# A Fourier filter and an expert layer on one core: three of eight sequences take their first-stage sums through DRAM

## The chip, the core and the metric

The kernel runs on one NeuronCore of a Trainium2 chip. The metric is the device time of one execution in microseconds. The kernel before took 454.48 us (the median of three runs, 452.73 to 454.86).

## The reference

The first half is a filter along the sequence, by Fourier transform; the second is a layer of experts that each keep at most 80 tokens.

```python
# x: 8 sequences x 2496 positions x 256 channels, f32; filt: 1249 x 256, complex
X = np.fft.rfft(x, axis=1)
y = np.fft.irfft(X * (filt_r + 1j * filt_i)[None], n=2496, axis=1)

x = y.reshape(19968, 256)
logits = x @ w_gate                          # 8 experts
expert_idx = argmax(logits); gate_w = its softmax probability
out = zeros((19968, 256))
for e in range(8):
    tok = the (at most 80) tokens of expert e with the largest gate_w
    out[tok] = gate_w[tok] * (relu(x[tok] @ w1[e]) @ w2[e])     # 256 -> 1024 -> 256
```

At most 640 of the 19968 rows of the output are not zero.

## The kernel before

Everything is float32 and runs on one core: TensorE for products and transposes, ScalarE and VectorE to take results out of the accumulators (PSUM), VectorE and GpSimd for the product with the filter. SyncE issues most DMAs, ScalarE's queue some, GpSimd's the gathers. The order of work is written out by hand in one loop (`tc.manual_schedule()`, from L824); each engine then works through its own instructions in order, and starts each as soon as what it waits for is there. SyncE computes nothing and runs ahead until a wait holds it.

The transform of length 2496 = 39 x 64 is done in two stages, and the kernel goes back only as far as it must: the gate's logits are worked out from the spectrum, and only the rows that are picked are turned back into tokens.

- **Stage 1** (`stage1`, L317) works on sequence `b` in 11 groups `k`. Line `j*21+g` of the 64 (j of 0 to 2, g of 0 to 20) is transformed over its 39 positions; three lines (the three values of j) go into one product by a block table `wf_t` of 117 x 120. A group has two such g, so four products: x is the stationary side (117 x 128 channels, twice), `wf_t` the moving one (120 columns). Group 10 has one g. Line 63 does not fit this order; for three sequences at once it is worked out with group 10 of sequences 0, 3 and 6, and kept in `left`. The results lie with channels on partitions and are copied into `t1` (L332), 80 x 64 to a channel, written with 64 floats between neighbours.
- **Transposes** (`transpose1`, L341): for each of 10 parts `u` of a sequence, four transposes turn `t1` so that lines and (real, imaginary) lie on partitions; ScalarE copies the result (`t2`, L349). They are issued `LEAD` = 2 steps ahead.
- **Stage 2** (`stage2`, L353): four products with the table `d_t` (L358), then two VectorE products with the filter `ft` (L366) and two GpSimd additions (L373).
- **Turn** (`turn`, L381): `LATE` = 2 steps later, four products with `gi` (identity and gate weights side by side, 136 columns, L386) turn the spectrum and give its gate sums; ScalarE copies it (L402).
- **Spectra kept** (`keep_spectrum`, L377): two parts at a time are stored to the DRAM tensor `yf` from ScalarE's queue, 512 KB each, five stores a sequence and 40 in all; those of sequence 0 go out one during each of sequences 1 to 5. The spectra of sequences 0 and 1 also stay in SBUF (`ysb`).
- **Zeros** (`put_zeros`, L194): 64 stores of 312 KB from SyncE fill the whole output with zeros. Only the scatter of the experts at the end depends on them.

One step `v` of the loop (L908) is part `u` of sequence `b`, with v = 10 b + u. It issues stage 2 of v, loads of x whose buffers are free (`put_x`, 7 buffers), the transposes of v + 2, one or two groups of stage 1 of a later part (`put_s1`), for the first sequence a transpose of the filter (`turn_filter`), a store of zeros, and the turn of v - 2. `fps` is a rotation of three PSUM buffers shared by stage 1, transposes and stage 2; `t1pool` holds two `t1`; `t2pool` has four buffers.

After the 80 steps come the choice of tokens, the turning back of the chosen rows (`turn_rows`, `add_rows`, which reload spectra from `yf`) and the experts (`Experts`), none of which the change edits. Two passes on TensorE make one f32 product, so counts in the profile are twice the products; a transpose is one pass.

Of the kernel before, what the change touches and what calls it, by code (L numbers as in the profile page):

```python
# [13 lines left out]
F32 = mybir.dt.float32  # L14
BF16 = mybir.dt.bfloat16
# [8 lines left out]
B, S, C = 8, 2496, 256  # L24
N = B * S
N1, N2 = 39, 64
NS, NQ = 20, 64
NU = NS // 2

NJ, NG = 3, 21  # L30
NB = NG // 2 + 1
JC = 4
# [9 lines left out]
def dft_tables():  # L42
    n1, n2 = np.arange(N1), np.arange(N2)
    s, q = np.arange(NS), np.arange(NQ)
    ph = 2 * np.pi * (np.outer(n1, s) % N1) / N1
    w = np.stack([np.cos(ph), -np.sin(ph)], 1)
    wf = np.zeros((N1, NJ, NJ, NS, 2))
    for j in range(NJ):
        wf[:, j, j] = w.transpose(0, 2, 1)

    k = np.array([[next(m for m in range(i, S, N1) if m % NQ == j) for j in q] for i in s])
    th = 2 * np.pi * (n2[:, None, None] * k % S) / S
    c, sn = np.cos(th), np.sin(th)
    d = np.zeros((2, N2, NS, 2, NQ))
    d[0, :, :, 0], d[1, :, :, 0] = c, sn
    d[0, :, :, 1], d[1, :, :, 1] = -sn, c

    two = np.where(s == 0, 1.0, 2.0) / S
    be = 2 * np.pi * (np.outer(q, n2) % NQ) / NQ
    back = np.zeros((2, NQ, 2, N2))  # L60
    back[0, :, 0], back[1, :, 0] = np.cos(be), -np.sin(be)
    back[0, :, 1], back[1, :, 1] = np.sin(be), np.cos(be)
    wi = np.zeros((4, SP, 2, N1, 4))
    for e in range(4):
        wi[e, :NS, 0, :, e] = (two * np.cos(ph)).T
        wi[e, :NS, 1, :, e] = (-two * np.sin(ph)).T

    n = (39 * n2[:, None] + 64 * n1) % S
    al = 2 * np.pi * (n.reshape(S, 1, 1) * k % S) / S
    rows = np.stack([np.cos(al), -np.sin(al)], 2) * two[:, None, None]  # L70

    frow = np.minimum(k, S - k).reshape(NU, 128).T
    fsig = np.where(k > S // 2, -1.0, 1.0).reshape(NU, 128).T
    f32 = np.float32
    return (wf.reshape(NJ * N1, -1).astype(f32), wi.reshape(4 * SP, 2, 4 * N1).astype(f32),
            d.reshape(128, NS, 128).astype(f32), back.reshape(128, 128).astype(f32),
            rows.reshape(S, NS * 128).astype(f32),
            np.ascontiguousarray(frow).astype(np.int32), np.ascontiguousarray(fsig).astype(f32))

# [2 lines left out]
def kernel(  # L82
# [11 lines left out]
    nc = tc.nc  # L94
# [10 lines left out]
    frow_dram = nc.inline_tensor(frow_host, name="frow_tbl")  # L105
    fsig_dram = nc.inline_tensor(fsig_host, name="fsig_tbl")

    NX = -(-max(E * cap - 128, 0) // 128)

    consts = ctx.enter_context(tc.tile_pool(name="consts", bufs=1))  # L110
    dpool = ctx.enter_context(tc.tile_pool(name="dram", bufs=1, space=DRAM))

    warm = consts.tile([128, 128], BF16, name="warm")
    nc.vector.memset(warm[:], 0.0)
    ident = consts.tile([128, 128], F32, name="ident")
    make_identity(nc, ident)
    ident_bf = consts.tile([128, 128], BF16, name="ident_bf")
# [16 lines left out]

    KC, KR = 8, 16
    PB, BB = 4096, 1 << 19
    K0 = K1 = 12
    cand = consts.tile([128, B, KC], F32, name="cand")  # L140
    cidx = consts.tile([128, B, KC], mybir.dt.uint32, name="cidx")
    code = consts.tile([128, B, KC], F32, name="code")
    cbase = consts.tile([128, B, KC], F32, name="cbase")
# [38 lines left out]

    NE, NY, NO = 3, 2, 3
    NWARM = 9
    yf = {b: dpool.tile([128, NS, C], F32, name=f"yf_{b}") for b in range(B)}
    ypool = ctx.enter_context(tc.tile_pool(name="spec", bufs=NY))
    ysb = {}
# [52 lines left out]
    with ExitStack() as actx:  # L240
# [17 lines left out]
        fspool = pool("fs", 3, within=bctx)  # L258
        ppool = pool("pp", 2, within=bctx)

        wf_t = tpool.tile([NJ * N1, NJ * 2 * NS], F32, name="wf_t")
        d_t = tpool.tile([128, NS, 128], F32, name="d_t")
        e_t = lpool.tile([128, 2 * N2], F32, name="e_t")
        wi_t = lpool.tile([4 * SP, 2, 4 * N1], F32, name="wi_t")
# [17 lines left out]
        def sign_filter(v):  # L282
            f = fst[:, v]
            for i in range(2):
                nc.scalar.activation(out=f[:, 2 + i, :], in_=f[:, 2 + i, :], func=AF.Copy,
                                     scale=fsig[:, 2 * v + i:2 * v + i + 1])
# [28 lines left out]
            st["x", b, ch] = xt  # L315

        def stage1(b, k):  # L317
            if k == 0:
                st["t1", b] = t1pool.tile([128, 4 * NS, N2], F32, name=f"t1_{b}", tag="t1")
            xt = st["x", b, 2 * k // JC]  # L320
            ps = fps.tile([128, 2, NJ, 4 * NS], F32, name=f"pa_{b}_{k}", tag="f")
            nk = 2 if k < NB - 1 or b % NJ == 0 else 1
            for i in range(nk):
                for cb in range(NDB):
                    nc.tensor.matmul(  # L325
                        out=ps[:, i, :, 2 * NS * cb:2 * NS * cb + 2 * NS],
                        lhsT=xt[0:NJ * N1, (2 * k + i) % JC, 128 * cb:128 * cb + 128],
                        rhs=wf_t[:], start=True, stop=True)
            full = 2 if k < NB - 1 else 1
            t1 = st["t1", b][:, :, 0:NJ * NG].rearrange("p a (j g) -> p g j a", j=NJ)  # L330
            copy = nc.vector.tensor_copy if b == 0 and k % 3 == 1 else nc.scalar.copy
            copy(out=t1[:, 2 * k:2 * k + full], in_=ps[:, 0:full])  # L332
            if k == 0 and b % NJ:
                nc.gpsimd.tensor_copy(out=st["t1", b][:, :, N2 - 1],
                                      in_=st["left"][:, b - min(b - b % NJ, B - NJ)])
            elif k == NB - 1 and b % NJ == 0:
                nc.scalar.copy(out=st["t1", b][:, :, N2 - 1], in_=ps[:, 1, b - min(b, B - NJ)])
                st["left"] = tpool.tile([128, NJ, 4 * NS], F32, name=f"left_{b}", tag="left")
                nc.vector.tensor_copy(out=st["left"][:], in_=ps[:, 1])

        def transpose1(b, u):  # L341
            t1 = st["t1", b]
            ps = fps.tile([128, 2, NDB, 128], F32, name=f"pt_{b}_{u}", tag="f")
            for i in range(2):
                for cb in range(NDB):
                    a = 2 * NS * cb + 2 * (2 * u + i)
                    nc.tensor.transpose(ps[:, i, cb, :], t1[:, a:a + 2, :].rearrange("p r n -> p (r n)"), ident[:])  # L347
            t2 = t2pool.tile([128, 2, C], F32, name=f"t2_{b}_{u}", tag="t2")
            nc.scalar.copy(out=t2[:].rearrange("p i c -> p (i c)"),  # L349
                           in_=ps[:].rearrange("p i c q -> p (i c q)"))  # L350
            st["t2", b, u] = t2

        def stage2(b, u):  # L353
            t2 = st.pop(("t2", b, u))
            ps = fps.tile([128, NDB, 2, 2, NQ], F32, name=f"pb_{b}_{u}", tag="f")
            for i in range(2):
                for cb in range(NDB):
# [19 lines left out]
        def keep_spectrum(b, u):  # L377
            src = st["ys"] if b >= NY else ysb[b][:, 2 * u - 2:2 * u + 2, :]
            nc.scalar.dma_start(out=yf[b][:, 2 * u - 2:2 * u + 2, :], in_=src)

        def turn(b, u):  # L381
# [18 lines left out]
            if b >= B - 2:  # L400
                nc.scalar.copy(out=zz, in_=pv[:, :, :, 128:ZW])
            nc.scalar.copy(out=dst.rearrange("p s (h w) -> p s h w", h=2), in_=pv[:, :, :, 0:128])  # L402
            if u % 2 == 1 and b > 0:
                keep_spectrum(b, u)
            if u == 4 and 0 < b < 6:
                keep_spectrum(0, 2 * b - 1)
            if b < B - 2:
                zz = zz[:, :, 0, :]
                nc.vector.tensor_copy(out=zz, in_=pv[:, :, 0, 128:ZW])  # L409
# [414 lines left out]
        with tc.manual_schedule():  # L824
# [5 lines left out]
                                    in_=moe_w_gate[128 * cb:128 * cb + 128, :])  # L830
            pre = fps.tile([128, 4, 128], F32, name="warm_ps", tag="f")
            for _ in range(NWARM):
                nc.tensor.matmul(out=pre[:], lhsT=warm[:], start=True, stop=True,
                                 rhs=warm[:].unsqueeze(1).to_broadcast([128, 4, 128]))
            xs = [(b, ch) for b in range(B) for ch in range(NCH)]
            s1 = [(b, k) for b in range(B) for k in range(NB)]

            held = dict(zip(range(NX0, NX0 + 14),
                            (0, 1, 2, 4, 5, 6, 8, 9, 11, 13, 15, 16, 17, 18)))
            free = [NX0]  # L840

            def put_x(v):
# [65 lines left out]
            for v in range(B * NU + LATE):  # L908
                b, u = divmod(v, NU)
                if b < B:  # L910
                    stage2(b, u)
                    if v + 2 < NU and v % 2 == 1:
                        sign_filter(v // 2 + 1)
                    put_x(v)
                    if v in (1, 3, 5):
                        load_d(2 + v // 2)
                    if v < 5:
                        load_filter(2 + (v + 1) // 2, (v + 1) % 2)
                    elif v == 5:
                        nc.gpsimd.dma_start(out=e_t, in_=e_dram.ap())  # L920
                        nc.gpsimd.dma_start(out=wi_t, in_=wi_dram.ap())
                    w = v + LEAD
                    if w < B * NU:
                        transpose1(*divmod(w, NU))
                    if v != 1:
                        put_s1()
                    if u == 3 or v in (6, 7):
                        put_s1()
                    if v + 2 < NU:
                        turn_filter(v // 2 + 1, v % 2)  # L930
                    if b > 0:
                        put_zeros(1)
                if v >= LATE:
                    turn(*divmod(v - LATE, NU))
                if b > 0 and u == LATE:
# [17 lines left out]
                if v == B * NU + 1:  # L953
                    turn_rows(0, 0)
                    turn_rows(0, 1)
            assert not (xs or s1 or early)
            put_zeros(len(zeros))
            bctx.close()
            st["yx"] = pool("yx", 1)
# [668 lines left out]
```

## Time and profile before

| | |
|---|---|
| median of the runs shown | 454.48 us (452.73 to 454.86) |
| the profiled execution | 455.56 us, span of its instructions 453.8 us |
| granted TensorE clock, mean | 0.989 |
| moved by DMA | 109.36 MB, 40091 packets, mean 241 GB/s |
| HBM read, written | 68.37 MB, 43.20 MB |
| loop of steps, first stage 2 to last | 26.4 to 286.7 us |

How to read the profile: a row of a group names the line of the kernel, the engine, the operation, output and inputs with their shapes and the count, then the busy time, the mean length of one, and the idle time of the engine before it with what ended it. TensorE's lengths overlap, since a pass starts before the one ahead of it has left the array; the distance from start to start is what a pass costs. PE is TensorE's products, PEld its loads of the stationary side, DVE is VectorE, ACT ScalarE, POOL GpSimd, SP SyncE, and a q behind a name is that engine's sequencer, which issues DMAs. In the 40 slices each digit is a tenth of the slice's time (9 is 90% or more). A row of waits reads: engine, tile and line that waited, what for, us in total, how often, the longest.

### The profile page before, as it was taken

The page shows a single profiled execution, that of the slowest core. Times are in us where ns is not written, and L with a number is a line of the kernel's source. Part 1 is how long each engine was busy: PE and PEld are TensorE (multiplying, and loading weights), DVE is VectorE, ACT ScalarE, POOL GpSimd, SP SyncE. Part 2 cuts the span into 40 slices and gives each one's busy share as a digit, 9 for nine tenths or more (in the row PEclk, how much of TensorE's full clock was granted, in tenths as well). Part 3 has the DMA queues.
Part 4 walks back from the last instruction along what each step waited for, and adds up shares of the span by engine and source line. Part 5 has one row for each costly group of instructions (what it writes and reads, how often), then busy time and mean ns, then how long its engine had stood idle before and what let it go on. Part 6 is the DMA issues. An engine that isn't in the chain of part 4 may idle for free. (4 is left out here: it accounts for less than half of the span.)

```text
span 453.8 us, 8686 instructions
## 1 busy us (share of the span) xinstructions
PE 435.1 (96%) x3369; PEld 409.0 (90%) x3369; DVE 193.2 (43%) x580; ACT 216.9 (48%) x362; POOL 180.5 (40%) x249
## 2 busy tenths in 40 slices
PE   8689999999999999999999999999999999999992
PEld 5689999999999999999999998888878888898881
DVE  1364554444674544764544789558320000111010
ACT  2556766666666666676666744342122232111110
POOL 7548633433444453454443465420645002022201
PEclk9989999999999999999999999999989999999998
DMA  7826545799887887888994222896987992799500
GB/s 198 233 69 206 169 115 136 261 366 375 310 253 240 300 284 251 262 264 260 333 399 163 96 94 93 276 369 272 347 345 264 366 378 64 274 370 371 183 12 20
DMA packets 40091, 109.36 MB, mean 241 GB/s; under 512 B 5336, under 2 KB 16158, under 8 KB 39272
## 3 DMA queue, kind: packets, MB, share of 16 engines
q1 hardware_dynamic: 29078, 75.81, 49.9%
q10 hardware_dynamic: 6466, 21.05, 11.8%
q0 software_dynamic: 4496, 11.85, 8.0%
q8 instruction: 29, 0.48, 0.4%
q14 instruction: 22, 0.18, 0.1%
HBM read 68.37 MB, written 43.20 MB: 246 GB/s over the span
## 5 line engine op out<-in xcount | busy, mean ns | idle before, releaser
L373 POOL TENSOR_TENSOR p<-p,p 128x256 f32<-128x256 f32 x154 | 110.4, 739 | 134.0 <-DVE p L366 76.9
L366 DVE TENSOR_TENSOR p<-pb,ft 128x512 f32<-128x512 f32 x160 | 102.1, 680 | 11.3 <-PE pb L358 11.2
L325 PE MATMUL pa<-wf_t,x 117*128 117x120 f32 x684 | 91.6, 282 | 3.1 <-DMA x<-in_x_dram 3.1
L332 ACT COPY t<-pa 128x480 f32<-128x480 f32 (+1 forms) x84 | 80.8, 969 | 28.4 <-PE pa L325 27.0
L325 PEld LDWEIGHTS pa<-wf_t,x 117*128 117x128 f32 x684 | 85.5, 197 | 4.9 <-DMA x<-in_x_dram 1.7
L386 PE MATMUL py<-gi,p 128*128 128x136 f32 x640 | 87.8, 280 | 1.3 <-POOL p L373 0.7
L358 PE MATMUL pb<-d_t,t 128*128 128x128 f32 x640 | 85.7, 277 | 0.4 <-ACT t L349 0.2
L386 PEld LDWEIGHTS py<-gi,p 128*128 128x128 f32 x640 | 79.7, 190 | 1.7 <-POOL p L373 1.0
L358 PEld LDWEIGHTS pb<-d_t,t 128*128 128x128 f32 x640 | 78.6, 193 | 1.5 <-ACT t L349 0.5
L349 ACT COPY t<-pt 128x512 f32<-128x512 f32 x80 | 46.9, 586 | 59.7 <-PE pt L347 57.8
L535 PE MATMUL po<-yb,wt 128*128 128x256 f32 x240 | 58.1, 387 | 0.9 <-ACT wt L528 0.9
L347 PE MATMUL pt<-ident,t 128*128 128x128 f32 x320 | 48.3, 274 | 2.6 <-issue 2.6
L535 PEld LDWEIGHTS po<-yb,wt 128*128 128x128 f32 x240 | 44.2, 194 | 6.2 <-ACT wt L528 1.1
L409 DVE COPY z<-py 128x16 f32<-128x16 f32 x60 | 11.2, 186 | 84.1 <-ACT ysp L402 56.1
L528 ACT COPY wt<-pw 128x512 f32<-128x512 f32 x39 | 22.8, 586 | 50.3 <-PE pw L523 42.4
L347 PEld LDWEIGHTS pt<-ident,t 128*128 128x128 f32 x320 | 37.8, 142 | 2.9 <-issue 2.9
L402 ACT COPY ysp<-py 128x512 f32<-128x512 f32 x60 | 35.5, 591 | 1.0 <-PE py L386 1.0
L1198 PEld LDWEIGHTS ph<-xs,w 128*128 128x128 f32 x256 | 29.6, 192 | 0.5
L1198 PE MATMUL ph<-xs,w 128*128 128x80 f32 x256 | 29.5, 274 | 0.0
L1213 PE MATMUL po<-w,hT 128*80 128x256 f32 x128 | 28.8, 379 | 0.0
L1213 PEld LDWEIGHTS po<-w,hT 128*80 128x80 f32 x128 | 18.6, 150 | 7.5
L523 PE MATMUL pw<-ident,gts 128*128 128x128 f32 x160 | 24.1, 276 | 0.6 <-issue 0.6
(207 smaller groups left out, 319.4 us busy)
## 6 DMA issues: line engine op xcount, KB each, us to landing
out_dram<-zero_t SPq DMA_DIRECT2D x64, 312.0 KB
x<-in_x_dram SPq DMA_DIRECT2D x40, 468.0 KB
w<-in_moe_w_dram SPq DMA_DIRECT2D x16, 1024.0 KB
yf<-ysp ACTq DMA_DIRECT2D x30, 512.0 KB
yb<-yf SPq DMA_DIRECT2D x6, 2560.0 KB
yf<-ys ACTq DMA_DIRECT2D x10, 512.0 KB
x<-in_x_dram SPq DMA_DIRECT2D x11, 117.0 KB
d_t<-d_tbl SPq DMA_DIRECT2D x5, 256.0 KB
```

Source lines behind the costliest of these rows:

```text
L325: nc.tensor.matmul(out=ps[:, i, :, 2 * NS * cb:2 * NS * cb + 2 * NS], lhsT=xt[0:NJ * N1, (2 * k + i) % JC, 128 * cb:128 * cb + 128], rhs=w ...
L332: copy(out=t1[:, 2 * k:2 * k + full], in_=ps[:, 0:full])
L347: nc.tensor.transpose(ps[:, i, cb, :], t1[:, a:a + 2, :].rearrange("p r n -> p (r n)"), ident[:])
L349: nc.scalar.copy(out=t2[:].rearrange("p i c -> p (i c)"), in_=ps[:].rearrange("p i c q -> p (i c q)"))
L358: nc.tensor.matmul(out=ps[:, cb, i], rhs=d_t[:, 2 * u + i, :], start=True, stop=True, lhsT=t2[:, i, 128 * cb:128 * cb + 128])
L366: nc.vector.tensor_tensor(out=pt, in0=ps[:].rearrange("p c s r q -> p (c s) r q"), in1=f.unsqueeze(2).to_broadcast([128, 2 * NDB, 2, NQ]), ...
L373: adder.tensor_tensor(out=yt[:, :, r, :], in0=yt[:, :, r, :], in1=pr[1][:, :, 1 - r, :], op=op)
L386: nc.tensor.matmul(out=ps[:, i, ZW * cb:ZW * cb + ZW], rhs=gi[:, cb, :], lhsT=yt[:, 2 * cb + i].rearrange("p r q -> p (r q)"), start=True, ...
L402: nc.scalar.copy(out=dst.rearrange("p s (h w) -> p s h w", h=2), in_=pv[:, :, :, 0:128])
L535: nc.tensor.matmul(pos[t][:, 0, 0:C], lhsT=wts[t, g // 2][:, g % 2, i, :], rhs=ybs[t][:, s, :], start=(s == 0), stop=(s == NS - 1))
L1198: nc.tensor.matmul(ph[:, fc // 4, fc % 4, 0:cap], lhsT=self.w1s[e][:, k, 128 * fc:128 * fc + 128], rhs=xs[:, k, :], start=(k == 0), stop=( ...
L1213: nc.tensor.matmul(po[0:cap, :], lhsT=hT[:, fc, :], rhs=self.w2s[e][:, fc, :], start=(fc == 0), stop=(fc == NFC - 1))
```

## The change

Sequences 1, 2 and 6 (`BOUNCE`) do stage 1 with the sides exchanged: `wf_t` is stationary and x moving, so that a group is two products of 256 columns rather than four of 120, and lines lie on partitions. ScalarE copies a group into a staging tile `sg` (from `t2pool`) and stores it from its own queue into a DRAM tensor `t_dram` of the sequence; `take` loads that tensor into `t1` in three pieces (48, 48 and 32 partitions) from SyncE, and stage 2 reads `t1` directly. These sequences have no transposes. The leftover line is stored with two small DMAs (`put_last`).

For the other five sequences `wf_t` has another order of columns, and is read with a stride so that the sums come out with lines innermost; the copy into `t1` then writes runs of 6 or 12 floats. The rows of `d_t` are put in the matching order (`places`).

Where the sequences that share a leftover line are of both kinds, it is worked out for both: one more product in sequence 0, two more in sequence 6.

The steps at which groups of stage 1 are issued are now a list (`s1_at`), and the steps of x loads differ a little. Zero stores are issued at other steps: 5 in steps 10 to 19, 34 in steps 20 to 47, none in 48 to 57, 18 in 58 to 69, and one a step from 70 on until all 64 are out. The spectra of sequences 0 and 1 are stored during sequences 2 to 6, two a sequence. The tile for the warm-up products shares memory with `cand`.

```diff
-    wf = np.zeros((N1, NJ, NJ, NS, 2))
+    wf = np.zeros((N1, NJ, 2, NJ, NS))
...
+    def places(a):
+        g = a[:, :NJ * NG].reshape(2, NJ, NG, NS, -1).transpose(2, 0, 1, 3, 4)
+        return np.concatenate([g.reshape(NJ * 2 * NG, NS, -1), a[:, -1].reshape(2, NS, -1)])
...
+    BOUNCE = (1, 2, 6)
...
+            def still(ps, i):
                 for cb in range(NDB):
                     nc.tensor.matmul(
-                        out=ps[:, i, :, 2 * NS * cb:2 * NS * cb + 2 * NS],
+                        out=ps[:, i, NM * cb:NM * cb + NM],
                         lhsT=xt[0:NJ * N1, (2 * k + i) % JC, 128 * cb:128 * cb + 128],
-                        rhs=wf_t[:], start=True, stop=True)
+                        rhs=wf_t[:].rearrange("p (a s) -> p s a", s=NS), start=True, stop=True)
+
+            def moving(ps, i):
+                nc.tensor.matmul(
+                    out=ps[0:NM, i], lhsT=wf_t[:],
+                    rhs=xt[0:NJ * N1, (2 * k + i) % JC, :], start=True, stop=True)
+
+            if b in BOUNCE:
+                ps = fps.tile([128, 2, C], F32, name=f"pa_{b}_{k}", tag="f")
+                for i in range(nk):
+                    moving(ps, i)
+                sg = t2pool.tile([128, 2, C], F32, name=f"sg_{b}_{k}", tag="t2")
+                nc.scalar.copy(out=sg[0:NM, 0:nk], in_=ps[0:NM, 0:nk])
+                if k == 0:
+                    t_dram[b] = dpool.tile([128, NS, C], F32, name=f"t_{b}")
+                p0 = 2 * NJ * 2 * k
+                nc.scalar.dma_start(
+                    out=t_dram[b][p0:p0 + 2 * NJ * full].rearrange("(i a) s c -> (a s) i c", i=full),
+                    in_=sg[0:NM, 0:full])
...
+                if k in (3, 7, NB - 1):
+                    takes.append((b, k))
+                return
...
-            copy(out=t1[:, 2 * k:2 * k + full], in_=ps[:, 0:full])
+            p0 = 2 * NJ * 2 * k
+            copy(out=t1[:, :, p0:p0 + 2 * NJ * full].rearrange("p a (i g) -> p a i g", i=full),
+                 in_=ps[:, 0:full].rearrange("p i (a g) -> p a i g", a=NDB * NS))
...
+        def put_last(b, src):
+            for r in range(2):
+                p0 = NS * (NJ * r + place3(b))
+                nc.scalar.dma_start(out=t_dram[b][128 - 2 + r], in_=src[p0:p0 + NS, :])
+
+        def take(v):
+            while takes and v >= NU * (takes[0][0] - 1):
+                b, k = takes.pop(0)
+                p0, p1 = {3: (0, 48), 7: (48, 96), NB - 1: (96, 128)}[k]
+                if k == 3:
+                    st["t1", b] = t1pool.tile([128, NS, C], F32, name=f"t1_{b}", tag="t1")
+                nc.sync.dma_start(out=st["t1", b][p0:p1], in_=t_dram[b][p0:p1])
...
-            t2 = st.pop(("t2", b, u))
+            t2 = (st["t1", b][:, 2 * u:2 * u + 2, :] if b in BOUNCE else
+                  st.pop(("t2", b, u)))
...
-            if u % 2 == 1 and b > 0:
+            if u % 2 == 1 and b >= NY:
                 keep_spectrum(b, u)
-            if u == 4 and 0 < b < 6:
-                keep_spectrum(0, 2 * b - 1)
+            if u in (4, 8) and NY <= b < 7:
+                keep_spectrum(u // 4 - 1, 2 * (b - NY) + 1)
...
+            s1_at = [0, 2, 3, 3, 4, 5, 5, 6, 6, 7]
+            s1_at += [8, 9, 10, 10, 11, 12, 12, 13, 14, 14, 15]
+            s1_at += [19, 20, 20, 21, 22, 22, 23, 24, 25, 26, 27]
+            s1_at += [29, 30, 30, 31, 32, 32, 33, 34, 35, 36, 37]
+            s1_at += sorted([*range(38, 48), 43])
+            s1_at += [48, 49, 49, 50, 51, 51, 52, 53, 53, 54, 55]
+            s1_at += sorted([*range(58, 68), 63])
...
+                    take(v)
                     put_x(v)
...
-                    if w < B * NU:
+                    if w < B * NU and w // NU not in BOUNCE:
                         transpose1(*divmod(w, NU))
-                    if v != 1:
-                        put_s1()
-                    if u == 3 or v in (6, 7):
+                    for _ in range(s1_at.count(v)):
                         put_s1()
...
-                    if b > 0:
-                        put_zeros(1)
+                    put_zeros(v % 2 if NU <= v < 20 else 1 + (v % 5 == 0) if 20 <= v < 48 else
+                              1 + v % 2 if 58 <= v < 70 else int(v >= 70))
```

## The prediction

> **What bounds the kernel now.** I read the engine sums and the slices first, then what TensorE waited for, then one step of the main loop on TensorE in order of time, then the same engine later, where its moving side is 256 columns wide, and last the loads on the DMA engines by stage.
>
> The page's engine sums, and TensorE's and the DMA engines' 40 slices:
>
> ```profile
> PE 435.1 (96%) x3369; PEld 409.0 (90%) x3369; DVE 193.2 (43%) x580; ACT 216.9 (48%) x362; POOL 180.5 (40%) x249
> ...
> PE   8689999999999999999999999999999999999992
> ...
> DMA  7826545799887887888994222896987992799500
> ```
>
> TensorE is full from the fourth slice to the last but one; every other engine is under half. Its longest waits:
>
> ```profile
> PE pa L325 <- DMA x<-in_x_dram: 3.1, 4, 1.3
> PE pt L347 <- issue: 2.6, 1, 2.6
> ```
>
> No wait in the loop is above 1.3 us: the loop costs what TensorE's passes cost. The timeline of TensorE, steps 10 and 11 (start, length, work; lengths overlap, so a price is the distance between starts):
>
> ```profile
> 63.03 1.05 PE L358 MATMUL pb<-d_t,t 128*128 128x128 f32 x8
> 63.93 0.60 PE L347 MATMUL pt<-ident,t 128*128 128x128 f32 x4
> 64.36 1.05 PE L325 MATMUL pa<-wf_t,x 117*128 117x120 f32 x8
> 65.25 1.10 PE L386 MATMUL py<-gi,p 128*128 128x136 f32 x8
> 66.19 1.05 PE L358 MATMUL pb<-d_t,t 128*128 128x128 f32 x8
> ```
>
> A step is stage 2 (0.90), four transposes (0.43), a group of stage 1 (0.89), turn (0.94): 3.16 us with no gap. One f32 product is two passes; a transpose is one. The same engine at 256 moving columns:
>
> ```profile
> 319.41 1.89 PE L535 MATMUL po<-yb,wt 128*128 128x256 f32 x8
> 321.14 0.60 PE L523 MATMUL pw<-ident,gts 128*128 128x128 f32 x4
> ```
>
> Eight passes of 256 columns take 1.73 us, 0.216 each; the passes of 120 above take 0.111 each.
>
> **The change, part by part.**
>
> *Transposes.* Sequences 1, 2 and 6 lose ten groups of four each: 30 x 0.43 = 12.9 us, all on TensorE, which is the path. ScalarE loses 30 copies of 0.59 us, which it had to spare.
>
> *Stage 1 of the three.* A full group was eight passes of 120 columns, 0.89 us; it becomes four passes of 256, 0.865. Over 30 groups that is 0.75 us less; half the products at twice the columns buys nothing more. The leftover line adds one moving product for sequence 0 (0.43) and two still ones for sequence 6 (0.44). Together +0.1. TensorE's sum: -12.8 us.
>
> *Stage 1 of the other five.* The product keeps its size, but its moving side, `wf_t`, is now read with neighbours 20 floats apart. Every moving operand of weight in the trace is read in order, so this has no row. At best it costs nothing: the 117x120 passes go at 0.111 us and those of 80 columns (L1198, 29 passes from 399.79 to 403.03) at 0.112, so what sets that pace is not the column count, and some column time is hidden. At worst it goes like the nearest strided rows, ScalarE's stores:
>
> ```profile
> L332 ACT COPY t<-pa 128x480 f32<-128x480 f32 (+1 forms) x84 | 80.8, 969 | 28.4 <-PE pa L325 27.0
> ...
> L349 ACT COPY t<-pt 128x512 f32<-128x512 f32 x80 | 46.9, 586 | 59.7 <-PE pt L347 57.8
> ```
>
> L349 writes in order, L332 with 256 bytes between neighbours (480-element copies in the timeline: 1.00). ScalarE copies 256 elements in order in 0.380 us (L426), so an element in order is (586-380)/256 = 0.80 ns and the fixed part 0.174 us; a strided one is (1000-174)/480 = 1.72 ns. At 1.72 ns a column a pass is 0.206 us, 0.095 more. There are 216 such products, 432 passes: 41 us. I take zero: the row that prices it is a store by another engine, while a TensorE pass already spends 0.93 ns on each of its 120 columns. I keep 41 us for the range.
> [...]
>
> *ScalarE's copies.* Of its 84 strided copies 51 stay, now writing runs of 6 to 12 in order, and 33 become plain ones: between 0.58 and 1.00 us each. 39 DMA issues of 0.33 us (L379's) are added, 13 us, where 17.7 us of transposed copies went. ScalarE works 44 of 68 us and 59 of 87 us in the middle stages (windows below) while TensorE has no gap, so TensorE hides it; without that cover the balance is still not above zero.
>
> *The trip through DRAM.* Each of the three sequences writes and reads back 2.62 MB. The ScalarE queue's row prices that:
>
> ```profile
> q10 hardware_dynamic: 6466, 21.05, 11.8%
> ```
>
> 11.8% of 453.8 us for 21.05 MB is 2.54 us of all 16 engines per MB; the SyncE queue's 49.9% for 75.81 MB is 2.99. So 15.7 MB is 40 to 47 us of DMA time. Is there room? By windows (length, ..., DMA share, GB/s):
>
> ```profile
> 26.00:59.90 33.90, 33.00 (x284) 32.41 (x284) 18.69 (x48) 23.01 (x35) 22.72 (x29) 0.98 0.49 144
> 59.90:128.00 68.10, 67.68 (x597) 67.24 (x596) 35.24 (x101) 44.50 (x68) 29.10 (x43) 1.00 0.79 270
> 128.00:215.00 87.00, 86.97 (x770) 86.77 (x769) 47.33 (x127) 58.94 (x90) 38.56 (x57) 1.00 0.84 266
> 215.00:286.70 71.70, 70.84 (x629) 69.87 (x628) 50.15 (x132) 43.33 (x85) 35.48 (x49) 1.00 0.51 190
> ```
>
> Busy: 16.6 + 53.8 + 73.1 + 36.6 = 180 of 260.7 us. After: 220 to 227 of about 251, 89%. It fits, and the 20 MB of zeros, which nobody reads in the loop, give way: only 5 zero stores stand in steps 10 to 19, none in 48 to 57, and SyncE, which runs ahead of TensorE, puts the last 25 behind sequence 6's last reading. The ten spectra of sequences 0 and 1 move to sequences 2 to 6, same count: nothing.
>
> *The wait it adds.* Stage 2 of a bounced sequence needs all of `t1`. The last leg, from the last group: copy 0.6, three issues 1.0, store, SyncE's issue 0.85 (L305's median 0.84), load of 655 KB (1.7 at 2.54 us per MB). For a store up to the start of its reader the trace has, on SyncE and on GpSimd:
>
> ```profile
> 376.02 0.34 SPq L547 DMA_DIRECT2D y_sel<-yr  x1
> ```
> ```profile
> 378.61 0.97 POOL L1168 DMA_INDIRECT xg<-y_sel,idxg  x1 [29.28 <-DVE xg L1166]
> ```
>
> 2.6 us, which I take twice: 0.6+1.0+2.6+0.85+1.7+2.6 = 9.4 us. Cover: sequence 1's last group is in step 7 and its stage 2 in step 10; between them stand a filter turn (0.43), a turn (0.94) and two steps without transposes (2 x 2.7): 6.8 us. So TensorE waits 2.6 us there. Sequence 2 has steps 15 to 20 (13 us), sequence 6 steps 55 to 60 (16 us): covered, at 89% of DMA.
> [...]
> Queued behind these readings on SyncE are loads of x: `take` waits for stores that ScalarE issues one step earlier, and the next chunk of sequence 1 or 2 goes only then. ScalarE's staging tiles share four buffers with the transposed sums, so a copy can wait for a store of two steps ago (6 us against about 3). For both I add 1 us (zero to 6).
>
> *Sum.* 455.56 (the profiled execution; its span 453.8) - 12.8 + 2.6 + 1 = 446.4; that execution is 1.08 above the median of 454.48, so 445. Own range of this case: 441 (no wait) to 452 (6 us of queueing more).
>
> **Rivals.**
>
> *The strided moving side costs (slower).* Place: stage 1 of sequences 0, 3, 4, 5, 7. Price up to 41 us: 445 + 41 = 486; at half that 465. It decides from 21 ns more a pass (9 us over 432 passes), that is at 1.09 ns a column where 0.93 is spent now. For it: ScalarE's strided store at twice the price, and TensorE without a gap to hide it in. Against: no strided read in the trace at all.
>
> *The DRAM trip lies open (near no change).* If legs take twice 9.4 us at 89% DMA load, the waits are 12 + 6 + 3 us before sequences 1, 2 and 6: the 12.8 are gone, about 455, 448 to 463 with part of it. For it: DMA shares of 0.79 to 0.84 in the loop already. Against: zeros make room, and early steps run at 0.49.
>
> *TensorE was not the bound there*, so that fewer passes change nothing: 454. The 3.16 us step without a gap speaks against it; I give it nothing of its own.
>
> **How the numbers follow.** Forecast 0.57, strided read 0.28, open trip 0.15 (half of it within 0.5%, half slower). A measurement of this kernel tells 0.5%, 2.3 us, from no change; so faster 0.57, same 0.08, slower 0.35. The range: from 440, just under the forecast's best, to 480, which takes in the open trip and the smaller half of the strided case; left out are the full strided price (some 0.15) and 0.04 below.
>
> **What would show it.** Right: transposes down from 320 to 200, the step at 2.7 us in sequences 1, 2 and 6, stage 1 of the rest still 0.89 us from start to start, a wait of 2 to 4 us of L432 for the DMA into `t1` near 60 us. Wrong: stage 1 groups of 1.1 to 1.7 us in sequences 0, 3, 4, 5 and 7 (strided read); waits on `t1` before sequences 2 and 6, or ScalarE waiting on its staging tiles (open trip); stage 1 waiting for x behind the readings.

## The result: slower by 15%, and the profile after

The changed kernel took 524.03 us (median of four runs, 521.89 to 526.25) against 454.39 (452.73 to 454.86): a ratio of 1.154, interval 1.148 to 1.160. The forecast of 445 us was wrong, and so was its range to 480. The profiled execution took 521.89 us, its span is 520.1, against 455.56 and 453.8.

The page of the changed kernel: the engine sums, TensorE's slices, the granted clock, the DMA engines' slices:

```profile
PE 474.5 (91%) x3127; PEld 434.6 (84%) x3127; DVE 192.6 (37%) x580; ACT 169.1 (33%) x331; POOL 178.9 (34%) x247
...
PE   8999478798999999999849999999998999999993
...
PEclk8999789898999999999979999999999999999998
DMA  7549677898777757767878996328979799199800
```

TensorE has 242 instructions fewer on record and is busy 39 us longer. Its slices (13 us each) now have holes at the fifth to eighth and at the twenty-first, and the granted clock is at 7 in the fifth and the twenty-first.

Two groups of the page, stage 1 with x stationary and stage 1 with x moving:

```profile
L333 PE MATMUL pa<-wf_t,x 117*128 117x120 f32 x428 | 101.1, 397 | 1.8 <-DMA x<-in_x_dram 1.4
...
L339 PE MATMUL pa<-x,wf_t 117*120 117x256 f32 x128 | 37.0, 423 | 13.5 <-ACT t L422 7.3
```

One pass of L333 lasts 397 ns, where the same pass lasted 282 with the table read in order. The timeline of TensorE of the changed kernel (start, length, work, in brackets the idle time before it):

```profile
52.93 1.05 PE L432 MATMUL pb<-d_t,t 128*128 128x128 f32 x8
61.57 1.12 PE L420 MATMUL pt<-ident,t 128*128 128x128 f32 x4 [7.58 <-ACT sg L348]
62.48 3.46 PE L339 MATMUL pa<-x,wf_t 117*120 117x256 f32 x8
65.77 0.60 PE L302 MATMUL pf<-ident,fst 128*128 128x128 f32 x4
...
136.66 1.92 PE L333 MATMUL pa<-wf_t,x 117*128 117x120 f32 x8
138.40 1.11 PE L460 MATMUL py<-gi,p 128*128 128x136 f32 x8
```

Three readings. At 136.66 a strided group takes 1.74 us from start to start, 0.218 a pass, where it was 0.89 and 0.111. At 54.0 TensorE stops for 7.6 us. And what follows the stop runs at half speed: the eight moving passes from 62.48 take 3.29 us, 0.41 each, where eight passes of 256 columns took 1.73 before.

What TensorE waited for, in order of size:

```profile
PE pt L420 <- ACT sg L348: 8.8, 2, 7.6
PE pa L339 <- ACT t L422: 7.3, 2, 7.0
PE pa L339 <- DMA x<-in_x_dram: 4.9, 2, 3.8
PE pf L302 <- ACT t L422: 3.8, 1, 3.8
PE pb L432 <- DMA t<-t: 2.3, 1, 2.3
```

Only the last is a wait for `t1`, the kind that the forecast's sum priced, at 2.6 us before sequence 1; this one falls before sequence 2. The first leads to ScalarE's timeline, still of the changed kernel:

```profile
51.06 0.32 ACTq L352 DMA_DIRECT2D t<-sg  x1
60.93 0.58 ACT L348 COPY sg<-pa 120x512 f32<-120x512 f32 x1 [9.90 <-DMA t<-sg]
```

A copy into a staging tile stands 9.9 us until an earlier store from such a tile has landed. ScalarE starts no other copy in those 9.9 us, so that no PSUM buffer comes free for TensorE's transposes, which wait 7.58. SyncE had issued the first reading of sequence 1 (`take`, 48 partitions) at 47.21, just before.

The DMA packets that the trace recorded show what held the stores. The 48 pieces of the reading, 20 KB each, were on the DMA engines from 48.2 to 55.7 us, 2.1 us apiece. From 47.6 to 54.6 us no data packet of ScalarE's queue moved, though stores had been issued at 48.32 and 51.06. Their last packets ended 10.8 and 10.4 us after their issue; those of the store issued at 61.55, with no reading on its way, 2.1 us after it. Meanwhile the engines were full and moved little. A window of the changed kernel during the reading, and one of the kernel before (length, then busy time of TensorE, its loads, VectorE, ScalarE and GpSimd, granted clock, DMA share, GB/s; packets that overlap count each, so that the share can pass 1):

```profile
48.00:54.00 6.00, 5.70 (x40) 4.85 (x40) 2.42 (x8) 2.64 (x6) 5.52 (x8) 1.00 1.08 173
```
```profile
101.00:105.00 4.00, 4.00 (x38) 4.00 (x37) 2.28 (x6) 1.94 (x3) 1.41 (x2) 1.00 0.93 363
```

### The profile page after: what moved, and what is told of

The parts are those of the page before. It is cut to its first block, busy times and chain, and to the rows that moved or that the text cites. A ratio compares the mean times of both kernels' runs of the same rounds, so it can differ in the third digit from the quotient of the medians.

```text
span 520.1 us, 8285 instructions
## 1 busy us (share of the span) xinstructions
PE 474.5 (91%) x3127; PEld 434.6 (84%) x3127; DVE 192.6 (37%) x580; ACT 169.1 (33%) x331; POOL 178.9 (34%) x247
## 3 DMA queue, kind: packets, MB, share of 16 engines
q10 hardware_dynamic: 14701, 28.92, 15.7%
## 5 line engine op out<-in xcount | busy, mean ns | idle before, releaser
L333 PE MATMUL pa<-wf_t,x 117*128 117x120 f32 x428 | 101.1, 397 | 1.8 <-DMA x<-in_x_dram 1.4
L460 PE MATMUL py<-gi,p 128*128 128x136 f32 x640 | 90.8, 286 | 1.3 <-POOL p L447 0.7
L460 PEld LDWEIGHTS py<-gi,p 128*128 128x128 f32 x640 | 88.0, 197 | 4.1 <-POOL p L447 1.1
L333 PEld LDWEIGHTS pa<-wf_t,x 117*128 117x128 f32 x428 | 84.5, 209 | 7.3 <-DMA x<-in_x_dram 1.9
L377 ACT COPY t<-pa 128x480 f32<-128x480 f32 (+1 forms) x51 | 27.7, 543 | 84.0 <-PE pa L333 77.8
L339 PE MATMUL pa<-x,wf_t 117*120 117x256 f32 x128 | 37.0, 423 | 13.5 <-ACT t L422 7.3
L422 ACT COPY t<-pt 128x512 f32<-128x512 f32 x50 | 29.1, 584 | 43.8 <-PE pt L420 30.7
L339 PEld LDWEIGHTS pa<-x,wf_t 117*120 117x120 f32 x128 | 23.8, 204 | 19.1 <-ACT t L422 8.3
L420 PE MATMUL pt<-ident,t 128*128 128x128 f32 x200 | 30.5, 276 | 9.4 <-ACT sg L348 8.8
L602 ACT COPY wt<-pw 128x512 f32<-128x512 f32 x39 | 22.7, 586 | 49.9 <-PE pw L597 41.3
L348 ACT COPY sg<-pa 120x512 f32<-120x512 f32 (+1 forms) x33 | 18.9, 573 | 42.4 <-PE pa L339 24.8
L420 PEld LDWEIGHTS pt<-ident,t 128*128 128x128 f32 x200 | 23.6, 142 | 9.9 <-ACT sg L348 9.2
```

The source lines that it names most:

```text
L333: nc.tensor.matmul(out=ps[:, i, NM * cb:NM * cb + NM], lhsT=xt[0:NJ * N1, (2 * k + i) % JC, 128 * cb:128 * cb + 128], rhs=wf_t[:].rearrang ...
L339: nc.tensor.matmul(out=ps[0:NM, i], lhsT=wf_t[:], rhs=xt[0:NJ * N1, (2 * k + i) % JC, :], start=True, stop=True)
L377: copy(out=t1[:, :, p0:p0 + 2 * NJ * full].rearrange("p a (i g) -> p a i g", i=full), in_=ps[:, 0:full].rearrange("p i (a g) -> p a i g", ...
L420: nc.tensor.transpose(ps[:, i, cb, :], t1[:, NS * cb + 2 * u + i, :], ident[:])
L422: nc.scalar.copy(out=t2[:].rearrange("p i c -> p (i c)"), in_=ps[:].rearrange("p i c q -> p (i c q)"))
L460: nc.tensor.matmul(out=ps[:, i, ZW * cb:ZW * cb + ZW], rhs=gi[:, cb, :], lhsT=yt[:, 2 * cb + i].rearrange("p r q -> p (r q)"), start=True, ...
```

## The experiments

The kernel before ran beside each set, at medians of 453.65, 449.17, 448.77 and 449.0 us; every ratio is against its own set.

**The strided moving side alone.** The kernel before, with its table's columns stored in another order and read back with a stride, so that the products are the same; h is the distance between neighbours, in floats:

```diff
+    wf = wf.reshape(NJ * N1, 20, -1).transpose(0, 2, 1)      # 20, or 4, or 2
...
-                        rhs=wf_t[:], start=True, stop=True)
+                        rhs=wf_t[:].rearrange("p (t h) -> p h t", h=20), start=True, stop=True)
```

Neighbours 80 bytes apart, as in the change:

> The kernel before, with one thing changed: the columns of the stage 1 table are stored in another order and read back with neighbours 20 floats (80 bytes) apart, so that the products are the same ones. No sequence goes through DRAM. Theory S (the strided moving side costs a second 0.109 us a pass, as the passes of 0.22 us after the change suggest): all 684 passes pay, 684 x 0.109 = +74 us, about 529 us. Theory D (the DRAM trip and its waits cost the time, the stride little): 454 us.

16 bytes apart (h=4):

> As the run with 20 floats, with neighbours 4 floats (16 bytes) apart. [...] S, if it grows with the distance: clearly less, 454 to 490. D: 454.

8 bytes apart (h=2):

> [...] S, if any step over one element costs: 529. D: 454.

Measured: 519.02 us, ratio 1.146 (1.142 to 1.149); 515.74, 1.137 (1.133 to 1.141); 454.25, 1.001 (0.999 to 1.003). The group of stage 1 on the three pages, in that order:

```profile
L326 PE MATMUL pa<-wf_t,x 117*128 117x120 f32 x684 | 163.0, 397 | 1.1 <-DMA x<-in_x_dram 1.0
```
```profile
L326 PE MATMUL pa<-wf_t,x 117*128 117x120 f32 x684 | 158.1, 392 | 1.4 <-DMA x<-in_x_dram 1.2
```
```profile
L326 PE MATMUL pa<-wf_t,x 117*128 117x120 f32 x684 | 90.3, 277 | 6.3 <-DMA x<-in_x_dram 6.2
```

65.4 us over 684 passes is 0.096 a pass at 80 bytes, 62.1 us or 0.091 at 16, nothing at 8. So it is no price per byte of distance: it is there in full at 16 bytes and absent at 8. From start to start a pass costs more than that: 0.107 in the changed kernel (0.218 - 0.111), and here at 80 bytes 0.110, as a group of stage 1 takes 1.77 us, 0.221 a pass:

```profile
141.00 1.94 PE L326 MATMUL pa<-wf_t,x 117*128 117x120 f32 x8
142.77 1.10 PE L387 MATMUL py<-gi,p 128*128 128x136 f32 x8
```

The whole kernel shows less because 96 of the 684 passes stand ahead of the loop, where TensorE of the kernel before waits 4.7 us anyway and that of this one 1.0: the first stage 2 starts at 29.4 us where it started at 26.4, 3.0 us for 96 passes. From there to the last stage 2 the kernel takes 322.0 us where it took 260.5, 0.105 for each of the other 588.

**The rest of the change, with the table in order.** The changed kernel with a second table `wf_s` in the order in which the stationary sequences read it:

```diff
+        wf_s = tpool.tile([NJ * N1, NM], F32, name="wf_s")
...
-                        rhs=wf_t[:].rearrange("p (a s) -> p s a", s=NS), start=True, stop=True)
+                        rhs=wf_s[:], start=True, stop=True)
```

> The changed kernel with a second copy of the stage 1 table in the order in which the five still sequences read it, so that no moving side is strided; all else as changed (one constant tile shares memory with another to make room, and one small load is added at the start). S: the 432 passes get their 0.109 us back, 524 - 47 = 477 us; the waits that are left (about 30 us of idle TensorE and a halved clock after them) are D's, 477 - 442 = 35 us. If the waits came only from the slower steps: about 445.

Measured 484.79 us, 1.069 (1.064 to 1.074). So the stride is 39 us of the 70. Some 47 were expected back; but 88 of the 432 passes stand ahead of the loop, and there the first stage 2 comes 2.7 us earlier with the table in order (26.3 for 29.0 us). The other 344 at 0.107 are 36.8 us, 39.5 together. The remainder is still 31 us slower than before, while TensorE has 12.8 us less to do. The two longest kinds of wait of this kernel:

```profile
PE pt L423 <- ACT sg L351: 9.1, 3, 6.9
PE pa L342 <- DMA x<-in_x_dram: 5.8, 2, 4.4
```

**Without any trip.** The same kernel with no sequence in `BOUNCE`: the new layout, the moved zeros, spectra, loads and steps of stage 1 remain.

```diff
-    BOUNCE = (1, 2, 6)
+    BOUNCE = ()
```

> The in-order kernel with no sequence through DRAM (an empty list of sequences): all the changed steps of zeros, spectra, x and stage 1 stay. If these moves cost nothing: 454 us. If they are part of the loss (zeros colliding with x): up to 470.

Measured 449.26 us, 1.000 (0.998 to 1.002). All that was moved costs nothing by itself; the 31 us come with the three sequences.

**How the sums are read back.** One load of all 128 partitions after the last group, in place of 48, 48 and 32:

```diff
-                if k in (3, 7, NB - 1):
+                if k == NB - 1:
...
-                p0, p1 = {3: (0, 48), 7: (48, 96), NB - 1: (96, 128)}[k]
+                p0, p1 = 0, 128
```

> The in-order kernel, reading a sequence's sums back in one load of 128 partitions after its last group, where it was three loads of 48, 48 and 32. Theory D1 (the loads into part of the partitions hold the DMA engines for long, the 1 KB stores of the staging tiles wait behind them, ScalarE waits for a tile and TensorE for ScalarE): the waits on staging go, TensorE waits some 7 us for the load before sequence 1: 450 to 460 us. Theory D2 (the stores are slow by themselves, four shared buffers are too few): 480 to 490 as without this edit.

Or the three loads, each cut in five along its rows, so that a partition's piece is 4 KB and not 20:

```diff
-                nc.sync.dma_start(out=st["t1", b][p0:p1], in_=t_dram[b][p0:p1])
+                for s0 in range(0, NS, 4):
+                    nc.sync.dma_start(out=st["t1", b][p0:p1, s0:s0 + 4, :],
+                                      in_=t_dram[b][p0:p1, s0:s0 + 4, :])
```

> The in-order kernel with each of the three loads cut into five along the free axis, so that a descriptor is 4 KB and not 20 KB; the same partitions and bytes. D1, if what holds the stores is the length of a descriptor: waits on staging mostly go, 450 to 465. D1, if it is that 32 or 48 partitions are served at a lower rate: nearly unchanged, 475 to 490. D2: unchanged, 485.

Measured 466.29 us, 1.037 (1.030 to 1.043), and 468.88, 1.045 (1.037 to 1.053). Against 1.069 both help, by some 15 and 11 us; both times lie between the ranges that the theories gave. That the cut loads help with the same 48 and 32 partitions says that few partitions are not the whole of it: long pieces are part of it. The packets agree: with pieces of 4 KB the two stores issued at 41.0 and 43.7, beside the first reading, landed after 6.2 and 5.2 us, where in the changed kernel it was 10.8 and 10.4. The partitions are part of it too. In the changed kernel readings into partitions 0 to 47 moved 117 to 141 GB/s, into 48 to 95 202 to 208, into 96 to 127 177 to 220; the one load of 128 moved 245 to 340, with pieces of the same 20 KB. The one load gives up its cover for this, as TensorE's longest wait in it shows:

```profile
PE pb L435 <- DMA t<-t: 18.3, 3, 8.5
```

**Staging tiles of their own**, three in a pool `sgp` (room taken from `fs` and `pp`), with the three loads and with the one:

```diff
-                sg = t2pool.tile([128, 2, C], F32, name=f"sg_{b}_{k}", tag="t2")
+                sg = sgpool.tile([128, 2, C], F32, name=f"sg_{b}_{k}", tag="sg")
```

> Sequences 1, 2 and 6 through DRAM, table in order, three loads each as the change has it, but with three staging tiles of their own. D2 (shared tiles are what turns slow stores into waits of TensorE): ratio from 1.069 to 1.035 or less. D1 (the loads of 32 and 48 partitions hold the stores for so long that three tiles are as short as four shared ones): 1.055 or more.

> As the run before, with one load of 128 partitions a sequence. From 1.037 the 8 us that TensorE waited behind staging go and the 18 us for the load stay: 1.015 to 1.022. If staging and load are one cause (stores late, so loads late): 1.00 to 1.01.

Measured 477.4 us, 1.062 (1.059 to 1.066), and 459.92, 1.025 (1.021 to 1.028). With three loads the tiles are not the trouble: ScalarE's waits for its staging stores fall from 22.7 to 8.9 us, but TensorE's wait moves on to x, 13.5 us over three waits, for SyncE's loads of x stand in one queue behind the readings (the first issued at 40.68, x at 41.11), and to `t1`, 7.1 over two. With one load the waits on staging tiles are gone, and the cost is down to what stands in this timeline of TensorE (one load, own tiles):

```profile
56.76 1.09 PE L464 MATMUL py<-gi,p 128*128 128x136 f32 x8
65.91 2.05 PE L436 MATMUL pb<-d_t,t 128*128 128x128 f32 x8 [8.06 <-DMA t<-t]
67.75 3.53 PE L343 MATMUL pa<-x,wf_t 117*120 117x256 f32 x8
71.12 1.09 PE L464 MATMUL py<-gi,p 128*128 128x136 f32 x8
```

SyncE had issued that load at 56.16; 2.6 MB are 9.75 us on their way. Stage 2 and the group after it take 5.21 us where they take 2.62 at full speed. The waits for `t1` in this kernel are 8.06, 7.76 and 2.53 us (18.3 together); the first two are each followed by such a stretch, with 2.6 and 2.5 us lost in them. 18.3 + 5.1 - 12.8 = 10.6, and the kernel is 10.9 us above before.

**One sequence alone**, the one with the most cover, with one load:

```diff
-    BOUNCE = (1, 2, 6)
+    BOUNCE = (6,)
```

> As the run with one load, with sequence 6 alone through DRAM. Ten groups of transposes less (4.3 us), two products more (0.4): 450 us if its trip of five steps is covered; 455 or more if not.

Measured 454.58 us, 1.011 (1.006 to 1.016). TensorE waits 4.0 us for `t1` and 1.7 for a staging tile. From here five variants. Stage 1 of sequence 6 done two steps earlier:

```diff
-            s1_at += [48, 49, 49, 50, 51, 51, 52, 53, 53, 54, 55]
+            s1_at += [48, 48, 49, 49, 50, 50, 51, 51, 52, 52, 53]
```

> The kernel with sequence 6 alone through DRAM (table in order, one load), its stage 1 at two groups a step, done in step 53 rather than 55. If TensorE waits for t1 only because the trip is longer than its cover: the wait of 4 us and the halved clock after it go, 1.1% slower becomes about the time of before (ratio 0.998 to 1.002). If the stores are what is slow (staging): the stores come closer together, ScalarE waits more, ratio 1.01 as without this edit or more.

No zeros in steps 38 to 47:

```diff
-                    put_zeros(v % 2 if NU <= v < 20 else 1 + (v % 5 == 0) if 20 <= v < 48 else
+                    put_zeros(v % 2 if NU <= v < 20 else 1 + (v % 5 == 0) if 20 <= v < 38 else
```

> The same kernel with sequence 6 alone, without the 12 zero stores of steps 38 to 47 (they come later, behind the load). If the trip is long because zeros share the DMA engines with the stores: waits on staging and on t1 shrink, ratio 1.000 to 1.005. If the zeros are not what is in the way: 1.011 as without this edit.

Own staging tiles, as above:

> The same kernel with sequence 6 alone, with three staging tiles of their own, beside the four buffers for transposed sums that they shared (room is made by two tiles for spectra where there were three and by three products where there were four). D2 (too few shared buffers): ScalarE's 9 us of waiting for stores mostly go, TensorE's 2 to 3 us behind it too, the last store leaves some 3 us earlier: ratio 1.002 to 1.006. If the buffers are not the reason: 1.011.

All three:

> All three edits together. If the waits were the whole loss, TensorE's sum is what is left: ten groups of transposes less (4.3 us), two products more (0.4): ratio 0.991 to 0.993, about 3.5 us faster than before. If something else costs time with a sequence through DRAM: 1.00 or above.

And the earlier groups with own tiles, the zeros left as the change has them:

> Sequence 6 alone through DRAM, table in order, one load, three staging tiles of its own and stage 1 done by step 53; the zeros stay where the change put them. If the two waits (staging, and the load behind its need) were the whole loss: the 4.0 us wait on t1 of the run with own staging and the halved clock after it go, ratio 0.990 to 0.994, about 3.5 us faster than before. If something else costs: 1.000 or above.

| sequence 6 alone | ratio (interval) |
|---|---|
| as is | 1.011 (1.006 to 1.016) |
| earlier groups | 1.012 (1.009 to 1.016) |
| fewer zeros | 1.009 (1.006 to 1.012) |
| own tiles | 1.003 (1.001 to 1.005) |
| all three | 1.008 (1.005 to 1.010) |
| earlier groups, own tiles | 0.999 (0.997 to 1.001) |

Earlier groups alone exchange one wait for another: the wait for `t1` is gone and this one is there instead,

```profile
PE pa L342 <- ACT t L425: 4.2, 1, 4.2
```

since groups that follow each other faster need staging tiles sooner (just before it a copy of ScalarE waits 4.5 us for a staging store to land). Only both together remove both. Taking zeros out of steps 38 to 47 alone makes no clear difference, and it pushes them into later steps: all three changes are slower than the two without it, 1.008 against 0.999. The profiles show where: with all three ScalarE waits 10.0 us in three places for stores of zeros to land (4.5, 3.0 and 2.5), and TensorE 4.3 us for ScalarE; with the zeros left alone no such wait is among ScalarE's. None of ScalarE's work needs the zeros. The longest of these waits ends with the issue of a store of spectra, and behind it stands the copy; SyncE issues 37 stores of zeros in a row at that time:

```profile
215.71 49.98 SPq L205 DMA_DIRECT2D out_dram<-zero_t  x37
```
```profile
264.56 0.33 ACTq L457 DMA_DIRECT2D yf<-ysp  x1
264.93 0.59 ACT L426 COPY t<-pt 128x512 f32<-128x512 f32 x1 [4.46 <-DMA out_dram<-zero_t]
```

The last variant, at 0.999, was expected at 0.990 to 0.994. No version tried beats the kernel before. The loop of steps, from the first stage 2 to the last, takes 260.3 us without any trip and 259.9 with this one. Its window in both profiles, and steps 50 to 60 in it (columns as above), first without any trip:

```profile
190.00:240.00 50.00, 49.80 (x442) 49.64 (x441) 25.33 (x66) 27.86 (x53) 22.30 (x33) 1.00 0.83 307
22.80:283.00 260.20, 258.02 (x2271) 255.83 (x2271) 152.23 (x408) 141.80 (x275) 125.49 (x175) 1.00 0.69 231
```

And with sequence 6:

```profile
190.00:240.00 50.00, 47.18 (x376) 44.35 (x375) 24.48 (x66) 23.61 (x44) 21.41 (x31) 1.00 0.92 323
22.80:283.00 260.20, 255.26 (x2195) 249.99 (x2194) 152.07 (x409) 135.85 (x264) 125.51 (x176) 1.00 0.75 252
```

In the loop TensorE is busy 2.8 us less with the trip, and idle 2.8 us more, nearly all of it in waits under 1 us between 190 and 240 us: what the transposes gave is taken back in small waits, at a DMA share of 0.92 for 0.83. The 2.8 us are 1.1 short of the 3.9 that the sum of passes gives; where that went the two profiles, which are of different sets, don't settle.

## Why the prediction was wrong, point by point

*Transposes and TensorE's sum: right.* Transposes fell from 320 to 200, and a moving group takes 0.87 us (87.14 to 88.01) as forecast. ScalarE's own work fell from 216.9 to 169.1 us, and its copies into `t1` became cheaper (0.56 us for 480 elements, just below the 0.58 to 1.00 forecast). The DMA volume rose by 15.7 MB, as worked out.

*Strided moving side: the step "I take zero" failed.* It cost 39 us of the time. The upper end of 41 us held for the time, but not for the reason given: a pass costs 0.107 more where 0.095 was the dearest case, so that the 432 passes are 46 us of TensorE's own time, of which some 7, ahead of the loop, don't lengthen the kernel. Two of the arguments for zero were wrong. That ScalarE's strided store is another engine's was no ground to discard it: its 0.095 lies near what TensorE's pass costs, though that is an agreement of two numbers and not shown to be one cause. That the 0.111 of a pass hides some column time was an inference from 80 and 120 columns at one price; if there is such a reserve, it hid nothing of the strided time at 16 and 80 bytes. The rival of 486 us was priced about right, by itself.
Why neighbours 8 bytes apart cost nothing (1.001) and neighbours 16 bytes apart nearly as much (1.137) as at 80 (1.146), the runs don't show.

*The trip: the terms for the wait and the queueing (2.6 + 1) were mis-sized more than tenfold.* With the table in order the kernel is 31 us above before, 44 above what TensorE's sum alone would give. The mechanism was named (a copy into a staging tile waits for a store, x loads stand behind `take`), its size was not: a store was taken to need about 3 us against the 6 in which its buffer comes round, and beside the first reading it needed 10.8; and it came not in one place but in a row.

The changed kernel's loop is 64.1 us longer than before (324.6 for 260.5). TensorE's waits above 1 us in it are 29.4 us, where before had none. To them come the stretches at half speed behind five of them (waits of 7.6, 7.0, 3.8, 3.8 and 2.3 us), 9.4 us by start-to-start distances. So: 36.8 for the stride in the loop + 29.4 + 9.4 - 12.8 = 62.8. The loop also starts 2.6 us later, which makes 65.4 of the 66.3 us between the spans.

What made the waits large was the reading, not the room on average: windows with holes show DMA shares of 0.77 (26 to 60 us) and 0.81 (60 to 128), less than the 0.89 that was allowed. But during the first reading nothing of ScalarE's queue moved for 7 us, as the packets above show, and x loads stood behind it on SyncE's own. One load and short pieces help by 15 and 11 us, own tiles remove the staging waits only with the one load, and what is left then is the wait for `t1`, in the sum above. Why ScalarE's queue stands still beside long pieces the runs don't show.

*The wait before sequence 1* was forecast at 2.6 us for `t1`. In the changed kernel it isn't seen: TensorE has been held up by 7.6 and 3.8 us before that point, and `t1` is there when stage 2 comes. With one load and own tiles it is 8.06, since all 2.6 MB then follow the last group.
The readings of 96 to 127, priced at 1.7 us in the sum, were on the engines for 3.0 to 3.7 us, at 177 to 220 GB/s; 48 to 95 moved 202 to 208, one load of 128 245 to 340, and 0 to 47 only 117 to 141. What sets these partitions apart the runs don't show.

*Sequences 2 and 6 covered: wrong as changed* (before sequence 2 waits of 3.8 us for x and 2.3 for `t1`; at sequence 6 one of 7.0 us for a copy of ScalarE that stood behind a staging store). *For sequence 6 it came right with own tiles and earlier groups* (no wait for `t1` left); sequence 2 was not tried so.

*Zeros, spectra, steps of stage 1: right.* 1.000 with all of them moved and no trip.

*The rivals.* Strided side and open trip were weighed as alternatives, one or the other. They are independent, and both came true. The open trip's waits of 12, 6 and 3 us lead to 463 by its own sum, so that 455 as its middle does not follow from them. By its own upper ends, 463 for the open trip and 41 for the stride, the far end was 504; that too falls short of 524, but 480 left the pair out altogether.

## What to carry to other kernels

Read a matmul's moving side in order: neighbours 8 bytes apart cost nothing here (1.001), 16 bytes (1.137) nearly as much as 80 (1.146). A change of layout that makes a copy cheaper on an idle engine and strides an operand on the full one was paid here with 39 us, and a second small table took them back. The round trip through DRAM cost 44 us above TensorE's sum where the forecast had 3.6: count the tiles that wait for a store to land (22.7 us of ScalarE's waiting with the table in order), the loads that stand in the same queues (13.5 us of TensorE's for x with own tiles), what a long-pieced reading does to both (10.8 us for a store of 2.1), and a stretch at half speed, which followed each of the 22 waits of 3.2 us or more that TensorE has in the loops here. When two risks of one change are independent, the range must hold both together.

## What the hardware showed that was not expected

A pass of 120 f32 columns costs 0.111 us with neighbours 4 or 8 bytes apart and 0.21 to 0.22 with 16 or 80.

After waits TensorE ran at half speed (eight passes of 256 columns in 3.3 to 3.5 us for 1.73), for up to some 6 us. The granted clock shows it: in the changed kernel it was 0.51 right behind the wait of 7.6 us and 1.00 after that, and 0.86 from 60 to 128 us as a whole (columns as in the windows above):

```profile
61.60:65.70 4.10, 4.10 (x12) 3.38 (x13) 1.56 (x5) 1.76 (x3) 1.40 (x2) 0.51 0.53 122
65.80:68.50 2.70, 2.70 (x26) 2.70 (x25) 1.20 (x4) 1.75 (x4) 0.00 (x0) 1.00 0.94 250
```
```profile
60.00:128.00 68.00, 55.22 (x340) 51.18 (x341) 25.84 (x78) 21.55 (x39) 21.13 (x30) 0.86 0.81 229
```

Each of the 22 waits of 3.2 us or more in the loop, in nine kernels, was followed by such a stretch. Of the waits from 1.9 to 2.7 us some were and some were not: the 2.3 us for `t1` in the changed kernel were followed by eight passes in 1.74 us for 0.89, the 2.53 us in the kernel with one load and own tiles by eight in 0.97. In the kernel with the table in order it even set in after two waits of 1.3 and 1.2 us, less than three us apart. What sets them apart the runs don't show.

And a store of 240 KB that takes 2.1 us from its issue to its last packet with no reading beside it took 10.8 beside a reading of 48 partitions in pieces of 20 KB on another queue.
